# Buffers and loads of the last rows' stacks, places of the bias copies, and low addresses for x's extra stacks, in a linear-attention block with a gated feed-forward part

## The chip, the cores and the metric

One core of one Trainium2 chip. The time is that of the device for one launch, in microseconds (us), lower is better; the number compared is the median over runs of the same kernel. Each engine of the core (PE for matmuls with PEld for its weight loads, DVE, ACT, POOL) works through its own list of instructions in order; SP issues most of the DMA transfers, in order as well.

## What is computed

```python
S, D, F, H = 2048, 576, 4608, 32
xn = layernorm(x)
q, k, v = split(xn @ wqkv)                       # 32 heads of 18
pq, pk = phi(q), phi(k)                          # phi(t) = (t > 0 ? t + 1 : exp(t)) + 1e-6
s = ((pq @ (pk.T @ v)) / (pq @ sum(pk) + 1e-6)) @ wo
g = silu(gelu(xn @ w1 + b1) @ w2 + b2)           # 576 -> 4608 -> 576
out = x + s * g
```

All in float32. The two big products, `xn @ w1` and its result `@ w2`, are nearly all of the work.

## The kernel before

**Numbers.** A product of float32 matrices is made of three matmuls: each operand is split into a high part that the PE takes as it is (`..h`, a cast on ACT) and a low part (`..l`, a subtraction on DVE), and high by high, high by low and low by high are added. On top of that, blocks of 2 by 2 are multiplied with seven products in place of eight, so operands are also sums and differences of blocks. Such sums are computed on POOL and DVE, split, and stored to DRAM for the second half of the rows (`op..` stores, `w..<-op` loads).

**Stages.** From 0 to about 283 us of the profiled execution run the layernorm, the projections and the attention; its result goes to DRAM. The rest is the feed-forward part: 18 *chunks*, two halves of the 2048 rows by nine pieces of F of 512 columns (`half`, `c`). A chunk has 28 *steps* of about 1.6 us of PE work. Steps 0 to 13 are two `Up` (the first product, seven each, into PSUM tiles `a`, `b`, `zy`, `e`). Steps 14 to 27 are the second product: seven products 1, 2, 7, 4, 5, 3, 6 of two steps each (`pm`, L1461), whose results DVE adds to `macc` (the sums of the output, which start from the bias `b2`). Between the two, ACT applies bias and gelu (`g`, L1307), and casts the h operands. For product i and half j of its depth these are tile `(i, j)`. Their buffers are five pairs of tiles, first written in a chunk so: h0 by (1,0) at step 7, h2 by (2,0) at step 9, h4 by (7,0) at step 10, h1 by (1,1) at step 11, h3 by (2,1) at step 12. `mid` is a tile of five blocks for intermediate sums of an `Up` (L1316, L1319, L1322) and of `W1`. `b<-e,mid` (L1325) is the sum that PE's step 12 (`e<-xSH,wb`) waits for, since it takes over the tile of `e`.

**Order.** On DVE, ACT, POOL and PE the program's order is kept. It comes from tables: `add(base + at, f)` puts a call of `f` at step `at` of a chunk. A list by steps decides thus what stands before what on an engine; a call at a negative step is one of the chunk before. SP's order is set by the scheduler. Each of its transfers uses one of eight semaphores in turn, so it starts only after the transfer eight places ahead has landed.

**Last rows.** D = 576 is 4 x 128 + 64. The last 64 rows of x and of the weights are stacked two blocks on top of each other, so that one more matmul closes a product: `xrest` (of x) against `w.rest(i)` (of the weights). The stacks are made from raw rows by class `Rest`: `hi` casts (L333), `lo` subtracts (L337), `sums` forms block sums of the raw rows on DVE (L354 or L356), `store` writes h and l to DRAM (L348), each twice over. There are two groups: the first has 3 blocks (128 x 384), the second, of the sums, 4 (128 x 512). Stacks 0 and 1 of the weights are made in the attention stage (`REST_PLAN`: round and slot of the four calls), the others in chunks 2, 3, 5 and 6 by `Rest2` (`plan_rest2`), which borrows h buffers: h4's high tile for the raw rows, h2 for the first group, h1 for the second. These instructions bear names such as `rs2Falseh1l`: stack 2, not of x, buffer h1, low part. Back from DRAM come x's stacks as `x_extra` (1 MB, four of seven; once for each half) and the weights' as `we` (448 KB for each `Up`, L1083).

**Memory.** Pools open from the low or the high end (`side="right"`) of the on-chip memory. The slot "mid" at a low address holds the attention's `scr` in the first stage, and becomes free when its last round is done with it; then it holds `mid`. `x_extra` and `we` lie on the right side.

**Biases.** `set_bias` copies `b2` on ACT into the four quarters of `macc` (L1279), in chunks 0 and 9.

Of the kernel before, what the change touches and what calls it, by code (L numbers as in the profile page):

```python
# [8 lines left out]
F32 = mybir.dt.float32  # L9
F32R = mybir.dt.float32r  # L10
# [5 lines left out]
P = 128  # L16
# [29 lines left out]
def linear_attention_gated_ffn(ctx, tc, x, wqkv, wo, w1, w1e, b1, w2, b2, out):  # L46
    nc = tc.nc
# [35 lines left out]
    def stage(cols, name):  # L83
        t = stg.tile([P, D], F32, tag="stg", name=name)
        return t[:, :cols]
# [25 lines left out]
    xp = ctx.enter_context(tc.tile_pool(name="xp", bufs=1, reuse_waits="tile"))  # L111
# [6 lines left out]
    scr = xp.tile([P, 2560], F32, tag="mid", name="scr")  # L118
# [7 lines left out]
    we_dram = [dram.tile([P, 4, 7, P], F32, name=f"we_dram{i}") for i in range(NB4)]  # L126
# [19 lines left out]
    class Weight:  # L146
# [8 lines left out]
        def rest(self, n):  # L155
            hs = slice(n * HD, (n + 1) * HD)
            return self.rh[:, hs], self.rl[:, hs]
# [157 lines left out]
    class Rest:  # L315
# [9 lines left out]
        def tiles(self, g):  # L325
            pool, bufs = rest_pool
            t = pool.tile([P, 2, 4 * P], F32R, tag="re", name=f"re{self.i}{self.of_x}{g}", bufs=bufs)
            return t[:, 0], t[:, 1]
# [258 lines left out]
    def add(step, fn, *args):  # L587
        plans.setdefault(step, []).append((fn, args))
# [19 lines left out]
    DV, GP = nc.vector, nc.gpsimd  # L608
# [85 lines left out]
    def plan_pair(p):  # L694
# [103 lines left out]
    rests, rest_pool = {}, (t1, 1)  # L798
    REST_PLAN = {
# [3 lines left out]
    }  # L803

    def load_rows(key):
# [14 lines left out]
    for p in range(1, NPAIR):  # L820
        plan_pair(p)
        base = p * NSP
# [22 lines left out]
    def q_tiles(r):  # L845
        return [r_bufs[(2 * r + s) % 4] for s in range(2)]
# [11 lines left out]
    base = NPAIR * NSP  # L858
# [173 lines left out]
    class W1:  # L1032
# [11 lines left out]
        def T(self, i):  # L1044

            a, b = slice(0, 2), slice(2, 4)
            f0, f1, src = self.f0, self.f1, self.src
            tt = EW1.tensor_tensor
            if i in (5, 6):
                at = (i - 5) * 2 * P  # L1050
                t = mid[:, 4, at : at + 2 * P] if self.n else scr[:, at : at + 2 * P]
                src[i] = t.rearrange("p (k c) -> p k c", k=2)
            if i == 5:
                tt(src[5], f1[:, a], f0[:, a], op=SUB)  # L1054
            elif i == 6:
                tt(src[6], f1[:, b], src[5], op=SUB)
            elif i == 7:
                src[7] = f1[:, a]
                tt(src[7], f1[:, b], f1[:, a], op=SUB)
            else:  # L1060
                src[4] = f0[:, b]
                tt(src[4], f0[:, b], src[6], op=SUB)
# [16 lines left out]

        def load_rest(self):  # L1080
            n = self.n % NP
            self.re = xe.tile([P, 7, P], F32R, tag="we", name=f"we{self.n}", bufs=2)
            nc.sync.dma_start(self.re.bitcast(F32), we_dram[n // 4][:, n % 4])  # L1083

        def rest(self, i):
            return self.re[:, W_REST[i]]

    W1_K = {"a": KM, "b": 2, 4: 2, 5: 2, 6: 2, 7: 2}

# [17 lines left out]
    W_REST = {1: 0, 2: 1, 3: 2, 5: 3, 4: 4, 6: 5, 7: 6}  # L1107
# [9 lines left out]
    w1t, w2_raw0 = {}, []  # L1117
# [5 lines left out]
    for r in range(NPAIR + 2):  # L1123
        base = (NPAIR + r) * NSP
# [3 lines left out]
        if r < NPAIR:  # L1128
            a, b = q_tiles(r)
# [15 lines left out]
        if 1 <= r < NPAIR:  # L1145
            a, b = q_tiles(r)
            at = base + 2 * (r == 2)
# [12 lines left out]
        if 3 <= r <= 7:  # L1160
            n = 2 * r + 3
# [25 lines left out]
        if 1 <= r < NPAIR:  # L1187
            for s in range(2):
                at = Attend(r - 2, s) if r >= 2 else None
# [14 lines left out]
        elif r == NPAIR:  # L1204
            w = w1t[0]
            at = Attend(r - 2, 0)
# [6 lines left out]
            at = Attend(r - 2, 1)  # L1213
# [12 lines left out]
        elif r > NPAIR:  # L1226
            for s in range(2):
                at = Attend(r - 2, s)
# [14 lines left out]

    gp = ctx.enter_context(tc.tile_pool(name="gp", bufs=1, side="right", reuse_waits="tile"))
    xe = ctx.enter_context(tc.tile_pool(name="xe", bufs=1, side="right", reuse_waits="tile"))
    x_extra = xe.tile([P, 4, 4, P], F32R, name="x_extra")

    def load_x_extra(i):
        nc.sync.dma_start(x_extra.bitcast(F32), xe_dram[i][:, :, :4])

    load_x_extra(0)
    for n in range(2):
        w1t[n].load_rest()
    for d, t in kept:
        nc.sync.dma_start(d, t)
    kept = None
    xrest = {k: t[:, at] for k, (t, at, _) in X_OVER.items()}
    xrest |= {k: x_extra[:, :, j] for j, k in enumerate(X_EXTRA)}
# [3 lines left out]
    tails = {}  # L1262
    macc = fl.tile([P, QH, 5, HD], F32, name="macc")
    C11, C12, C21, C22, U1 = range(5)
    mid = xp.tile([P, 5, 512], F32, tag="mid", name="mid")
    m1_sb, u1_sb, u2_sb = (mid[:, i, :] for i in range(3))

    BIAS = (C11, C22)
# [71 lines left out]
    class Rest2(Rest):  # L1340
# [5 lines left out]
            return gp.tile([P, 512], F32R, tag=tag, name=f"rs{self.i}{self.of_x}{tag}", bufs=1)  # L1346

        def tiles(self, g):
            return [self.tile(f"h{2 - g}{v}") for v in "hl"]

    REST_CHUNK = {2: (2, False), 3: (3, False), 5: (1, True), 6: (4, False)}

    def plan_rest2(base, key):
        def load():
            rests[key] = Rest2(*key)

        add(base + 0, load)
        for at, what, *args in (
            (2, "hi", 0), (3, "lo", 0), (3, "sums", DV), (4, "store", 0), (5, "hi", 1), (6, "lo", 1), (7, "store", 1),
        ):  # L1360
            add(base + at, lambda what=what, args=args: getattr(rests[key], what)(*args))

# [175 lines left out]
    def finish_load(t, h, tiles):  # L1538
        b, q = divmod(t - 8, QH)
        cs = slice(h * HD, (h + 1) * HD)  # L1540
        nc.sync.dma_start(tiles[0], c_dram[b, :, q, h])
        nc.sync.dma_start(tiles[1], s_dram[t, :, cs])
        nc.sync.dma_start(tiles[2], x[t * P : (t + 1) * P, cs])

    def finish(t, h, tiles):
        ct, st, xt = tiles
        nc.gpsimd.tensor_tensor(st, ct, st, op=MUL)  # L1547
        nc.gpsimd.tensor_tensor(st, st, xt, op=ADD)
        nc.sync.dma_start(out[t * P : (t + 1) * P, h * HD : (h + 1) * HD], st)
# [60 lines left out]
    NS = 28  # L1610
# [3 lines left out]
    def plan_w1(add, w, base, T, hi, lo):  # L1614
        for table, what in ((T, w.T), (hi, w.hi), (lo, w.lo)):
            for i, at in table.items():
                add(base + at, what, i)
# [3 lines left out]
        hi={"a": 0, 6: 1, 7: 2, 5: 3, "b": 4, 4: 4},  # L1621
        lo={"a": 0, 6: 1, 7: 2, 5: 3, "b": 4, 4: 4},
# [3 lines left out]
        hi={"a": 24, 6: 25, 7: 26, 5: 26, "b": 27, 4: 27},  # L1626
        lo={"a": 24, 6: 25, 7: 26, 5: 26, "b": 27, 4: 27},
# [10 lines left out]
        hi={  # L1638
            (1, 0): 7, (2, 0): 9, (7, 0): 10, (1, 1): 11, (2, 1): 12, (7, 1): 15, (4, 0): 16,
            (4, 1): 17, (5, 1): 18, (5, 0): 19, (6, 0): 20, (3, 0): 21, (3, 1): 22, (6, 1): 23,  # L1640
        },
        lo={
            (1, 0): 9, (2, 0): 10, (7, 0): 11, (1, 1): 12, (2, 1): 13, (7, 1): 15, (4, 0): 16,
            (4, 1): 17, (5, 1): 18, (5, 0): 19, (6, 0): 20, (3, 0): 21, (3, 1): 22, (6, 1): 23,
        },
# [11 lines left out]
    for step in range(n_chunks):  # L1657
        half, c = divmod(step, NC)
        base = step * NS
        plain = step == n_chunks - 1  # L1660
        h = HOps(c)
        if c == 0:
            if half:
                add(base + 5, load_bias, nc.gpsimd)
            for at, m in zip((10, 11, 13, 14) if half else (5, 6, 7, 8), (C11, C21, C22, C12)):
                add(base + at, set_bias, m)
        if half == 0:
            plan_w1(add, w1t[2 * step + 1], base, **P1)
# [7 lines left out]
            if step == 0:  # L1676
                for i, at in W2_SUMS_FIRST.items():
                    add(at, w2t[0].load, i)
        if half == 0 and c in REST_CHUNK:
            plan_rest2(base, REST_CHUNK[c])  # L1680
        if half == 0 and c < NC - 1:
            add(base + 0, make, W1, w1t, 2 * step + 2)
            add(base + 4, make, W1, w1t, 2 * step + 3)
# [56 lines left out]
        if half == 1 and 1 <= c <= 8:  # L1740
            for k in range(2):
                tiles = {}
                def load(k=k, t=7 + c, tiles=tiles):
                    tiles[0] = finish_tiles(k)
                    finish_load(t, k, tiles[0])
                add(base, load)
                add(base + 4, lambda k=k, t=7 + c, tiles=tiles: finish(t, k, tiles[0]))
# [12 lines left out]
        for j in range(CF // 2):  # L1760
            n = 2 * step + j
# [55 lines left out]
```

## Time and profile before

| what | value |
|---|---|
| median of 3 runs | 1130.23 us (1130.0 to 1131.81) |
| profiled execution, its time / its span | 1133.79 us / 1132.1 us |
| granted PE clock, mean | 0.99 |
| PE busy | 1101.4 us, 97% |
| PEld, DVE, ACT, POOL busy | 90%, 73%, 46%, 40% |
| DMA | 295.02 MB, mean 261 GB/s |
| chain that ended last | PE 82%, DMA 6%, DVE 5%, ACT 4% |

How to read it. A busy time counts an engine's own instructions. The chain is the row of work that set the end, followed back from the last instruction. In an answer by time a row gives start and length in us, the engine, the line, output and inputs, and in brackets how long the engine had been idle and what released it. "DMA x<-y" as a releaser is a transfer that had to land. The granted clock is the share of full speed that the chip let PE have; PE's busy time contains what a lower clock adds.

### The profile page before, as it was taken

What the parts mean: (1) busy time and instruction counts of PE and PEld (TensorE: products, weight loads), DVE (VectorE), ACT (ScalarE), POOL (GpSimd) and SP (SyncE); (2) the same over time, 40 slices, a digit from 0 to 9 for tenths busy, and PEclk for the clock granted to TensorE, in tenths of its full rate; (3) what the DMA queues carried; (4) which work ended last, traced back from release to release, by engine and by line L of the source; (5) the groups of instructions that cost most, each with busy time, mean ns of one, the idle gap of its engine ahead of it and who ended that gap; (6) DMA issues with size and microseconds to landing.
All of it is one profiled execution on the core that took longest, in us unless ns stands there. A gap on an engine that the chain in (4) does not pass through costs nothing.

```text
span 1132.1 us, 18955 instructions
## 1 busy us (share of the span) xinstructions
PE 1101.4 (97%) x6888; PEld 1014.0 (90%) x6888; DVE 822.8 (73%) x1284; ACT 516.7 (46%) x945; POOL 454.3 (40%) x423
## 2 busy tenths in 40 slices
PE   8999999999899989999898999999999999999998
PEld 8999999999698877989788898898998988989988
DVE  6777477996687868788888888675574664755776
ACT  7776455554635434444444435443243242332342
POOL 6854524555345333452524444234132342341310
PEclk9999999999999989999999999999999999999999
DMA  5989838888978969697887969997767667767343
GB/s 203 322 285 335 279 89 282 288 324 288 375 251 295 321 206 348 229 355 230 295 308 240 354 170 360 388 346 251 267 213 234 217 221 225 220 219 223 101 152 115
DMA packets 115867, 295.02 MB, mean 261 GB/s; under 512 B 12221, under 2 KB 31421, under 8 KB 113727
## 3 DMA queue, kind: packets, MB, share of 16 engines
q1 hardware_dynamic: 110207, 282.32, 70.5%
q0 software_dynamic: 4992, 10.32, 5.3%
q8 instruction: 54, 0.88, 0.3%
q10 hardware_dynamic: 576, 1.18, 0.3%
q14 instruction: 38, 0.31, 0.1%
HBM read 180.39 MB, written 108.66 MB: 255 GB/s over the span
## 4 chain that ended last, share of the span: by engine, by line
PE 82%; DMA 6%; DVE 5%; ACT 4%; issue 2%; POOL 0%; SPq 0%; DVEq 0%; ACTq 0%; POOLq 0%
PE pm L1461 34%; PE e L1299 8%; PE zy L1299 8%; PE a L1299 8%; PE pl L477 5%; PE b L1299 4%; PE ps_s L997 4%; PE e L421 2%; PE a L421 2%; PE z L421 2%; PE pd L1576 2%; PE ps_kva L530 1%; DMA we_dram<-rs2Falseh1l 1%; PE b L421 1%; DMA w__8337<-op 1%
## 5 line engine op out<-in xcount | busy, mean ns | idle before, releaser
L1027 ACT CAST h_h<-g 128x512 fp32r<-128x512 f32 x204 | 120.5, 621 | 158.2 <-PE pm L1461 138.9
L1030 DVE TENSOR_TENSOR h_l<-g,h_h 128x512 fp32r<-128x512 f32 x204 | 160.2, 785 | 10.3 <-ACT g L1307 7.4
L1469 DVE TENSOR_TENSOR macc<-macc,pm 128x576 f32<-128x576 f32 x136 | 102.2, 751 | 39.7 <-PE pm L1461 39.6
L1299 PE MATMUL a<-xH,wa 128*128 128x512 f32 x288 | 102.0, 395 | 0.0
L1471 DVE TENSOR_TENSOR macc<-pm,macc 128x576 f32<-128x576 f32 x98 | 74.1, 757 | 25.7 <-PE pm L1461 24.1
L1429 POOL TENSOR_TENSOR mid<-g 128x512 f32<-128x512 f32 x34 | 44.5, 1308 | 105.7 <-ACT g L1307 105.6
L1307 ACT ACTIVATE g<-b,b1c 128x512 f32<-128x512 f32 x36 | 24.8, 689 | 126.0 <-DVE b L1325 125.9
L1299 PE MATMUL e<-xSH,wb 128*128 128x512 f32 x144 | 53.7, 414 | 14.7 <-DVE b L1325 14.6
L1316 ACT COPY mid<-a 128x512 f32<-128x512 f32 x36 | 21.2, 589 | 97.7 <-PE a L1299 97.7
L1299 PEld LDWEIGHTS a<-xH,wa 128*128 128x128 f32 x288 | 54.0, 187 | 12.1 <-ACT mid L1316 0.8
L1423 POOL TENSOR_TENSOR g<-g 128x512 f32<-128x512 f32 x34 | 49.6, 1460 | 32.3 <-DVE h_l L1030 30.9
L1319 DVE TENSOR_TENSOR mid<-b,mid 128x512 f32<-128x512 f32 x36 | 24.7, 685 | 46.1 <-ACT h_h L1027 20.7
L1426 POOL TENSOR_TENSOR g<-g 128x512 f32<-128x512 f32 x34 | 51.7, 1519 | 12.5 <-DVE h_l L1030 11.1
L1299 PE MATMUL a<-xL,wa 128*128 128x512 f32 x144 | 56.2, 390 | 0.0
L1547 POOL TENSOR_TENSOR fin1l<-fin1h,fin1l 128x288 f32<-128x288 f32 x8 | 6.5, 808 | 118.6 <-DMA fin1l<-s_dram 61.8
L1299 PE MATMUL zy<-xH,w 128*128 128x512 f32 x144 | 51.8, 401 | 0.0
L1299 PE MATMUL b<-xSH,w 128*128 128x512 f32 x144 | 50.4, 390 | 0.0
L1299 PE MATMUL zy<-xSH,w 128*128 128x512 f32 x144 | 50.3, 390 | 0.0
L1299 PE MATMUL e<-xSH,w 128*128 128x512 f32 x144 | 50.3, 390 | 0.0
L1299 PEld LDWEIGHTS e<-xSH,wb 128*128 128x128 f32 x144 | 28.3, 196 | 23.8 <-DVE b L1325 17.5
L1420 POOL TENSOR_TENSOR g<-g 128x512 f32<-128x512 f32 x34 | 47.5, 1398 | 2.7
L1054 POOL TENSOR_TENSOR mid<-w1raw 128x256 f32<-128x256 f32 x17 | 13.9, 820 | 85.5 <-DMA w1raw<-w 52.1
(974 smaller groups left out, 3694.1 us busy)
## 6 DMA issues: line engine op xcount, KB each, us to landing
op<-w SPq DMA_DIRECT2D x72, 256.0 KB
w<-op SPq DMA_DIRECT2D x72, 256.0 KB
we<-we_dram SPq DMA_DIRECT2D x36, 448.0 KB
w2raw<-w SPq DMA_DIRECT2D x10, 1152.0 KB
op<-w2o SPq DMA_DIRECT2D x19, 576.0 KB
w1raw<-w SPq DMA_DIRECT2D x18, 512.0 KB
op_a<-wa SPq DMA_DIRECT2D x18, 512.0 KB
wa<-op_a SPq DMA_DIRECT2D x18, 512.0 KB
```

Of the source, the lines that this page charges most:

```text
L421: nc.tensor.matmul(ps, st, mv, start=first and n == 0, stop=n == len(seq) - 1, skip_group_check=True,)
L477: nc.tensor.matmul(self.ps[n], st, self.wk(hl, k, n), start=(i == 0), stop=(i == n_all - 1))
L997: nc.tensor.matmul(self.ps[h], st[:, k, :], w[:, k, h * HD : (h + 1) * HD], start=(i == 0), stop=(i == len(self.seq) - 1),)
L1027: nc.scalar.copy(pair[0], src)
L1030: eng.tensor_tensor(pair[1], src, pair[0].bitcast(F32), op=SUB)
L1299: nc.tensor.matmul(ps.rearrange("p (c j) -> p c j", c=4), st, mv, start=first and n == 0, stop=n == len(seq) - 1, skip_group_check=True,)
L1420: tt(src[5, pr], A(1, 1), A(1, 0), op=SUB)
L1423: tt(src[6, pr], src[5, pr], A(0, 0), op=ADD)
L1426: tt(src[3, pr], src[6, pr], A(0, 1), op=SUB)
L1461: nc.tensor.matmul(ps[:, q, :HD], hs[p][st][:, cs], m[:, p, :], start=(n == 0 and i not in CHAIN), stop=(n == len(seq) - 1), skip_group_ch ...
L1469: nc.vector.tensor_tensor(dst, dst, src, op=SUB)
L1471: nc.vector.tensor_tensor(dst, src, dst, op=ADD)
```

## The change

Four parts, as the diff has them.

1. `Rest2` takes h1 for the first group and h3 for the second (before: h2 and h1). Its raw rows are asked for four steps before the chunk (before: at step 0), its first store comes at step 3, ahead of the sums (before: 4), the second at step 6 (before: 7). `store`, `hi`, `lo`, `sums` themselves stay.
2. The four bias copies of chunk 0 go from steps 5, 6, 7, 8 to 10, 11, 13, 14, where chunk 9 has its own.
3. A tile `low` of 20 blocks of 128 takes the low slot. Its first 16 blocks are `x_extra`; the last four hold, two for each of two `Up` in turn, two of the seven blocks of `we` (those of products 1 and 2). The other five stay on the right side. So a `load_rest` is two transfers, 128x256 and 128x640, in place of one of 128x896; there are 36 of these loads. `mid` moves to the right side, and the first W1's sums go to a staging tile, since `scr` was their place.
4. `REST_PLAN` starts the stacks 0 and 1 of the weights about a round earlier in the attention stage.

```diff
@@ the attention stage
-        (0, False): ((10, 12), (11, 6), (12, 6), (13, 6)),
-        (1, False): ((12, 12), (13, 6), (14, 6), (15, 6)),
+        (0, False): ((9, 12), (10, 11), (11, 6), (12, 6)),
+        (1, False): ((11, 12), (12, 11), (13, 6), (14, 6)),
@@ W1.T
             if i in (5, 6):
+                if i == 5:
+                    self.tmp = mid[:, 4] if self.n else stage(4 * P, "w1t0")
                 at = (i - 5) * 2 * P
-                t = mid[:, 4, at : at + 2 * P] if self.n else scr[:, at : at + 2 * P]
+                t = self.tmp[:, at : at + 2 * P]
@@ W1.load_rest, W1.rest
-            self.re = xe.tile([P, 7, P], F32R, tag="we", name=f"we{self.n}", bufs=2)
-            nc.sync.dma_start(self.re.bitcast(F32), we_dram[n // 4][:, n % 4])
+            a = xe.tile([P, 5, P], F32R, tag="we", name=f"we{self.n}", bufs=2)
+            b = low[:, 16 + 2 * (n % 2) :][:, :2]
+            nc.sync.dma_start(b.bitcast(F32), we_dram[n // 4][:, n % 4, :2])
+            nc.sync.dma_start(a.bitcast(F32), we_dram[n // 4][:, n % 4, 2:])
+            self.re = a, b
...
-            return self.re[:, W_REST[i]]
+            at = W_REST[i]
+            return self.re[1][:, at] if at < 2 else self.re[0][:, at - 2]
@@ after the attention
-    x_extra = xe.tile([P, 4, 4, P], F32R, name="x_extra")
+    low = xp.tile([P, 20, P], F32R, tag="mid", name="low")
+    x_extra = low[:, :16].rearrange("p (c k) j -> p c k j", k=4)
...
     load_x_extra(0)
-    for n in range(2):
-        w1t[n].load_rest()
+    mid = xe.tile([P, 5, 512], F32, name="mid")
+    w1t[0].load_rest()
     for d, t in kept:
         nc.sync.dma_start(d, t)
+    w1t[1].load_rest()
...
-    mid = xp.tile([P, 5, 512], F32, tag="mid", name="mid")
@@ Rest2.tiles
-            return [self.tile(f"h{2 - g}{v}") for v in "hl"]
+            return [self.tile(f"h{1 + 2 * g}{v}") for v in "hl"]
@@ plan_rest2
-        add(base + 0, load)
+        add(base - 4, load)
-            (2, "hi", 0), (3, "lo", 0), (3, "sums", DV), (4, "store", 0), (5, "hi", 1), (6, "lo", 1), (7, "store", 1),
+            (2, "hi", 0), (3, "lo", 0), (3, "store", 0), (3, "sums", DV), (5, "hi", 1), (6, "lo", 1), (6, "store", 1),
@@ the chunks
-            for at, m in zip((10, 11, 13, 14) if half else (5, 6, 7, 8), (C11, C21, C22, C12)):
+            for at, m in zip((10, 11, 13, 14), (C11, C21, C22, C12)):
...
-        if half == 0 and c in REST_CHUNK:
-            plan_rest2(base, REST_CHUNK[c])
+        if half == 0 and c + 1 in REST_CHUNK:
+            plan_rest2(base + NS, REST_CHUNK[c + 1])
```

What stands in a row on an engine. DVE in chunk 2, around the two low parts of stack 2 (`rs2False..`), before; `w_..` are low parts of weights, L1325, L1332 and L1336 the sums of an `Up`:

```order
L1325 TENSOR_TENSOR b4_4701<-e4_4703,mid_3677 128x512
L1030 TENSOR_TENSOR w5_5_4766<-mid_3677,w5_5_4766 128x256
L1030 TENSOR_TENSOR w2_2__4771<-w2raw2_4351,w2_2__4771 128x576
L337 TENSOR_TENSOR rs2Falseh2l_4754<-rs2Falseh4h_4719,rs2Falseh2h_4753 128x384
L356 TENSOR_TENSOR rs2Falseh4h_4719<-rs2Falseh4h_4719 128x128 x4
L1030 TENSOR_TENSOR wb_5_4790<-w1raw5_4293,wb_5_4790 128x256
L1030 TENSOR_TENSOR w4_5_4792<-w1raw5_4293,w4_5_4792 128x256
L1030 TENSOR_TENSOR w2_2__4800<-w2s7_2_4305,w2_2__4800 128x576
L1332 TENSOR_TENSOR e4_4703<-e4_4703,mid_3677 128x512
L1336 TENSOR_TENSOR zy4_4702<-zy4_4702,mid_3677 128x512
L1030 TENSOR_TENSOR w2_2__4836<-w2raw2_4351,w2_2__4836 128x576
L337 TENSOR_TENSOR rs2Falseh1l_4820<-rs2Falseh4h_4719,rs2Falseh1h_4819 128x512
```

and now (the kernel's later lines have moved down by seven):

```order
L1332 TENSOR_TENSOR b4_4710<-e4_4712,mid_3661 128x512
L337 TENSOR_TENSOR rs2Falseh1l_4755<-rs2Falseh4h_4628,rs2Falseh1h_4754 128x384
L356 TENSOR_TENSOR rs2Falseh4h_4628<-rs2Falseh4h_4628 128x128 x4
L1030 TENSOR_TENSOR w5_5_4780<-mid_3661,w5_5_4780 128x256
L1030 TENSOR_TENSOR w2_2__4785<-w2raw2_4357,w2_2__4785 128x576
L1030 TENSOR_TENSOR wb_5_4799<-w1raw5_4298,wb_5_4799 128x256
L1030 TENSOR_TENSOR w4_5_4801<-w1raw5_4298,w4_5_4801 128x256
L1030 TENSOR_TENSOR w2_2__4809<-w2s7_2_4310,w2_2__4809 128x576
L1339 TENSOR_TENSOR e4_4712<-e4_4712,mid_3661 128x512
L1343 TENSOR_TENSOR zy4_4711<-zy4_4711,mid_3661 128x512
L337 TENSOR_TENSOR rs2Falseh3l_4827<-rs2Falseh4h_4628,rs2Falseh3h_4826 128x512
L1030 TENSOR_TENSOR w2_2__4846<-w2raw2_4357,w2_2__4846 128x576
```

The first low part and the four sums have moved up in front of two weight subtractions, to stand right behind `b<-e,mid`; the second low part has changed places with one weight subtraction.

SP in chunk 3, among the stores of the weights: `op..` are stores of split weight operands, `w1raw` and `w2s` loads of raw weights and raw sums for later chunks. Before:

```order
L1024 DMA op_5_5289<-w_7_5286 128x512
L1024 DMA op_1_5294<-w_3__5291 128x1152
L1024 DMA op_b<-wb_5310 128x512
L1024 DMA op_4_5318<-w_7_5312 128x512
L1024 DMA op_7_5323<-w_3__5320 128x1152
L348 DMA we_dram_109<-rs3Falseh2h 128x2x384
L348 DMA we_dram_109<-rs3Falseh2l 128x2x384
L1038 DMA w1raw_5327<-w 128x1024
L1377 DMA w2s_4_5342<-w 128x576
L1024 DMA op_3_5359<-w_3__5356 128x1152
L348 DMA we_dram_109<-rs3Falseh1h 128x2x512
L348 DMA we_dram_109<-rs3Falseh1l 128x2x512
```

and now:

```order
L348 DMA we_dram_109<-rs3Falseh1h 128x2x384
L348 DMA we_dram_109<-rs3Falseh1l 128x2x384
L1024 DMA op_5_5305<-w_7_5302 128x512
L1024 DMA op_1_5310<-w_3__5307 128x1152
L1024 DMA op_b<-wb_5321 128x512
L1024 DMA op_4_5329<-w_7_5323 128x512
L1024 DMA op_7_5334<-w_3__5331 128x1152
L1038 DMA w1raw_5336<-w 128x1024
L1384 DMA w2s_4_5351<-w 128x576
L348 DMA we_dram_109<-rs3Falseh3h 128x2x512
L348 DMA we_dram_109<-rs3Falseh3l 128x2x512
L1024 DMA op_3_5371<-w_3__5368 128x1152
```

The first two stores of the stack (128x2x384) stand in front of five `op` stores that they stood behind; the second two (128x2x512) have passed one `op` store, and still stand behind `w1raw` and `w2s`.

ACT in chunk 0, around the four copies into `macc` (`e`, `zy`, `a`, `b` are PSUM tiles of the two `Up`, `h_h` the high parts of h), before:

```order
L1307 ACTIVATE g<-e_3683,b1c 128x512
L1279 COPY macc<-macc 128x3x288
L1307 ACTIVATE g<-zy_3682,b1c 128x512
L1279 COPY macc<-macc 128x4x288
L1316 COPY mid<-a_3809 128x512
L1279 COPY macc<-macc 128x3x288
L1027 CAST h_h<-g 128x512
L1279 COPY macc<-macc 128x4x288
L1027 CAST w_0__3837<-w2raw_3434 128x576
L1027 CAST w_0__3851<-w2raw_3434 128x576
L1027 CAST h_h<-g 128x512
L1307 ACTIVATE g<-b_3810,b1c 128x512
```

and now:

```order
L1027 CAST w_0__3837<-w2raw_3434 128x576
L1027 CAST w_0__3851<-w2raw_3434 128x576
L1027 CAST h_h<-g 128x512
L1314 ACTIVATE g<-b_3811,b1c 128x512
L1286 COPY macc<-macc 128x3x288
L1027 CAST h_h<-mid 128x512
L1314 ACTIVATE g<-a_3810,b1c 128x512
L1286 COPY macc<-macc 128x4x288
L1027 CAST h_h<-g 128x512
L1314 ACTIVATE g<-e_3813,b1c 128x512
L1027 CAST h_h<-g 128x512
L1314 ACTIVATE g<-zy_3812,b1c 128x512
```

The four copies stand no more between `zy` of the first `Up` and the cast of the weights, but after the gelu of `b` of the second `Up`, two of them ahead of the cast of (1,1).

## Prediction

> **What bounds the kernel now.** I read the page first: the span, and the row of the granted clock in 40 slices of 28.3 us.
>
> ```profile
> span 1132.1 us, 18955 instructions
> PEclk9999999999999989999999999999999999999999
> ```
>
> PE is the bound nearly everywhere, so only places where PE stands still or runs slowly can be gained. The 8 near 400 us says that the clock fell there. Next I cut the span at the starts of the feed-forward chunks, read from the chain (each run of `pm` products ends where the next chunk starts). The rows are chunks 0, 2, 3, 4, 5, 6 and 9; columns: stretch, length, busy time of PE, PEld, DVE, ACT, POOL, granted clock, DMA share, GB/s.
>
> ```profile
> 282.87:333.25 50.38, 46.66 (x266) 41.51 (x265) 36.05 (x54) 27.92 (x50) 18.94 (x18) 0.97 0.89 316
> 378.18:431.75 53.57, 48.42 (x268) 43.36 (x267) 39.94 (x62) 22.41 (x43) 19.63 (x19) 0.94 0.79 272
> 431.75:481.89 50.14, 47.17 (x268) 41.90 (x267) 40.26 (x62) 22.32 (x43) 20.63 (x19) 0.97 0.81 285
> 481.89:526.83 44.94, 44.94 (x267) 40.79 (x267) 37.63 (x56) 21.32 (x41) 20.43 (x19) 1.00 0.82 283
> 526.83:577.21 50.38, 47.03 (x267) 41.75 (x267) 41.67 (x62) 22.41 (x43) 20.81 (x19) 0.97 0.84 288
> 577.21:627.65 50.44, 47.06 (x267) 41.80 (x267) 41.60 (x62) 22.41 (x43) 20.34 (x19) 0.97 0.84 285
> 717.53:763.88 46.35, 45.24 (x267) 40.80 (x267) 31.52 (x41) 22.46 (x32) 16.24 (x12) 1.00 0.98 367
> ```
>
> Chunk 4 is a full one, 44.94 us with PE never idle. Over it the others have 5.44 (chunk 0), 8.63, 5.20, 5.44, 5.50 (chunks 2, 3, 5, 6) and 1.41 (chunk 9). Each excess has two parts: PE idle (chunk 2: 53.57 - 48.42 = 5.15) and PE busy longer at a fallen clock (48.42 - 44.94 = 3.48). So every stall of some us is paid again: 1.7 us in chunk 0, 2.2 in 3, 2.1 in 5 and 6. Chunks 2, 3, 5 and 6 are those with the last rows' stacks: 24.77 us in all. Their waits, on ACT (chunk 2 twice, 3 twice, 5, 6):
>
> ```profile
> 398.99 0.62 ACT L1027 CAST h_h<-g 128x512 fp32r<-128x512 f32 x1 [4.14 <-DMA we_dram<-rs2Falseh2h]
> 405.32 0.62 ACT L1027 CAST h_h<-g 128x512 fp32r<-128x512 f32 x1 [3.91 <-DMA we_dram<-rs2Falseh1h]
> 451.60 0.62 ACT L1027 CAST h_h<-g 128x512 fp32r<-128x512 f32 x1 [3.18 <-DMA we_dram<-rs3Falseh2h]
> 457.85 0.62 ACT L1027 CAST h_h<-g 128x512 fp32r<-128x512 f32 x1 [2.88 <-DMA we_dram<-rs3Falseh1h]
> 552.59 0.62 ACT L1027 CAST h_h<-g 128x512 fp32r<-128x512 f32 x1 [1.18 <-DMA xe_dram<-rs1Trueh1h]
> 603.33 0.62 ACT L1027 CAST h_h<-g 128x512 fp32r<-128x512 f32 x1 [1.37 <-DMA we_dram<-rs4Falseh1h]
> ```
>
> A stored stack still occupies the buffer in which the next h is wanted. The low part of the second stack lands later yet, as the chain shows for chunks 2 and 3 (start, us): at 406.53 and 459.05.
>
> ```profile
> 397.01 9.52 DMA we_dram<-rs2Falseh1l
> 450.85 8.20 DMA we_dram<-rs3Falseh1l
> ```
>
> **The stacks, chunk 2.** Two stalls. The first, at step 12, is DVE's. These rows are DVE's of chunk 2, then the one of chunk 4 that answers to 398.89:
>
> ```profile
> 386.41 0.42 DVE L1030 TENSOR_TENSOR w<-mid,w 128x256 fp32r<-128x256 f32 x1 [1.05 <-ACT w L1027]
> 387.66 0.55 DVE L337 TENSOR_TENSOR rs2Falseh2l<-rs2Falseh4h,rs2Falseh2h 128x384 fp32r<-128x384 f32 x1
> 388.24 1.27 DVE L356 TENSOR_TENSOR rs2Falseh4h<-rs2Falseh4h 128x128 f32<-128x128 f32 x4
> 393.88 1.40 DVE L1030 TENSOR_TENSOR w__4836<-w2raw,w__4836 128x576 fp32r<-128x576 f32 x1 [1.81 <-ACT w__4836 L1027]
> 395.21 1.77 DVE L337 TENSOR_TENSOR rs2Falseh1l<-rs2Falseh4h,rs2Falseh1h 128x512 fp32r<-128x512 f32 x1
> 398.89 0.69 DVE L1325 TENSOR_TENSOR b<-e,mid 128x512 f32<-128x512 f32 x1
> 499.64 0.70 DVE L1325 TENSOR_TENSOR b<-e,mid 128x512 f32<-128x512 f32 x1 [0.31 <-PE e L1299]
> ```
>
> `b<-e` runs 17.75 us after the start in chunk 4 and 20.71 after it in chunk 2: 2.96 late. The order puts the first low part and the sums (0.55 + 1.27) into the 1.05 us wait, and the second low part (1.77) into the 1.81 us wait. Added 3.59, filled 2.86: about 0.7 us late, of which `e<-xSH,wb` on PE bears some 0.5 (2.96 late made a stall of about 2.4). I take 0.3 for chunks 2 and 3. In 5 and 6 DVE has 1.7 us more to do (41.67 against 39.94): between 0.3 and 1.9, and 0.6 taken, since DVE waits elsewhere too.
>
> The first store goes to buffers wanted at step 11 and passes five transfers in the queue; that wait ends. The second is closer. Its buffer moves from step 11 to step 12, so from product 1 to product 2, two of 28 steps or 3.2 us later. But it goes on the way hardly sooner: the queue still puts it behind the raw weights and `w2s`, each transfer waits until the eighth before it has landed, and only one store of 0.6 MB is no longer ahead of it. In this stretch the transfers run without a gap (first the queue's row of that store, then 384 to 388 us):
>
> ```profile
> 395.72 0.45 SPq L1024 DMA_DIRECT2D op<-w__4836  x1
> 384.00:388.00 4.00, 4.00 (x19) 3.27 (x18) 2.22 (x5) 2.61 (x6) 0.00 (x0) 1.00 1.03 406
> ```
>
> 0.6 MB at 406 GB/s is 1.5 us, so I let both halves land 1.5 us sooner: chunk 2 at 403.8 and 405.0. When does PE want them? Chunk 9 shows it: there PE stopped five matmuls into product 1 (163 of 168 come after), which begins half a chunk, 22.5 us, after 717.53, at 740.0, and wanted the low part some 0.65 us later.
>
> ```profile
> 738.52 1.15 ACT L1279 COPY macc<-macc 128x1152 f32<-128x1152 f32 x1
> 740.22 1.61 DVE L1030 TENSOR_TENSOR h_l<-g,h_h 128x512 fp32r<-128x512 f32 x1 [0.85 <-ACT h_h L1027]
> 741.88 22.00 PE pm L1461 x163
> ```
>
> So product 2's low part is wanted at 22.5 + 3.2 + 0.65 = 26.35 after the start, plus the 0.3 of step 12: 404.8 in chunk 2. The buffer is free at 405.0 and the subtraction takes 0.7: 0.9 late. In chunk 3: landed at 459.05 - 431.75 = 27.3, less 1.5, plus 0.7, is 26.5 against 26.65: 0.1 taken, for scatter. Chunk 6 I put at 0.2, chunk 5 at 0. Ends: nothing; or no sooner landing at all (rival 1). ACT casts that h some 3 us before PE wants it and stands still for that long at most; behind it lie `g<-zy` and the h of product 7, wanted 3.2 us later still.
>
> No stall left is near those that made the clock fall. After the change: 1.2, 0.4, 0.6 and 0.8 us of 24.77; gain 21.8. The number of loads, casts, sums and stores stays.
>
> **Bias copies of chunk 0.** First and last of four on ACT, then DVE:
>
> ```profile
> 295.41 0.91 ACT L1279 COPY macc<-macc 128x864 f32<-128x864 f32 x1
> 299.64 1.17 ACT L1279 COPY macc<-macc 128x1152 f32<-128x1152 f32 x1
> 298.46 0.69 DVE L1319 TENSOR_TENSOR mid<-b,mid 128x512 f32<-128x512 f32 x1 [3.07 <-ACT mid L1316]
> 301.42 1.38 DVE L1030 TENSOR_TENSOR w__3837<-w2raw,w__3837 128x576 fp32r<-128x576 f32 x1 [2.27 <-ACT w__3837 L1027]
> 305.06 0.69 DVE L1325 TENSOR_TENSOR b<-e,mid 128x512 f32<-128x512 f32 x1
> ```
>
> `b<-e` comes 22.2 us after 282.87, 4.4 later than in chunk 4, and the four copies are about 4.2 of ACT's time ahead of it. Moved, they leave one extra weight subtraction (about 1.2, against chunk 4) there: 0.6 at step 12. At steps 10 to 14 two copies lie ahead of an h of product 1, as in chunk 9, whose rows stand above and whose excess is 1.41, 1.2 of it this stop. So 5.44 becomes 1.9: 3.5 gained (ends: nothing left, 5.4; as long a stop as before, 0). Chunk 9 has its copies there already and keeps its 1.41.
>
> **The passage to the feed-forward part.** The queue, the chain, ACT, PE's first use:
>
> ```profile
> 261.27 0.52 SPq L1249 DMA_DIRECT2D x_extra<-xe_dram  x1
> 263.91 7.71 DMA op<-w2o
> 271.68 4.17 DMA w1raw<-w
> 275.93 0.62 ACT L1027 CAST wa<-w1raw 128x512 fp32r<-128x512 f32 x1 [4.30 <-DMA w1raw<-w]
> 278.31 0.54 PE L997 MATMUL ps_s<-kw_h,th 128*128 128x288 f32 x2 [1.18 <-ACT th L971]
> L1299 PEld LDWEIGHTS a<-x_extra,we x1: 186/186/186, 284.0 to 284.0; 128*128 128x128 f32 x1
> ```
>
> `x_extra` (1 MB, 2.6 us at 400 GB/s) leaves its place ahead of the `op` stores and a `we` part of 0.33 MB takes it: 1.8 us sooner for what follows, so ACT's 4.30 shrinks and PE's 1.18 goes: 1.2 gained. `x_extra` now starts after the raw weights; two `w1raw` of 0.5 MB, `w2raw` of 1.2 and `x_extra`, 3.2 MB from about 271 on, are 8 us, landing at about 280 against 282.8 wanted. If the margin of 2.8 is wrong by as much again, some 3 us are lost. The `re1False` stores that leave the last round cost or give nothing: ahead of that gap PE waits for nothing there.
>
> **36 more DMAs** (each `we` in two). SP's issue takes 0.3 to 0.5 us each (261.27: 0.52), at most 18 us of queue time over 18 chunks, a us in each; PE never waits for `we` in chunk 4, so I take 0, with ends of 0 and the 2 us of rival 2. The Trainium skill ("SBUF — State Buffer", The DMA setup-cost knee) fits a transfer as about 2 us plus its bytes at 436 GB/s and so advises the largest single transfers. By that the split would add 2 us to each, 4 in a chunk. The trace disagrees for a full queue: transfers of 0.25 to 0.6 MB went through at 406 GB/s together, where the fit gives a lone one of 0.26 MB about 100.
>
> **The sum.** 1.2 + 3.5 + 21.8 = 26.5. The profiled execution took 1133.79 us (span 1132.1), 3.56 over the median of 1130.23; the gain should carry over, so 1103.7, stated as 1104 (span about 1105.6).
>
> **Rivals.** 1. The second stacks land no sooner, since the queue is bound by bytes. Late by my rule: 2.4 in chunk 2, 1.4 in 3, and, with the low part landing 1.2 after the high one as in 2 and 3 and DVE's 0.6, 0.7 in 5 and 1.1 in 6; in all 5.6 against 1.2 taken, so 1108; with the clock falling behind each for 1.7, 1115. For it: the gapless 1.03 share. Against: the store no longer ahead. The Trainium skill ("TensorE: Matmul & The Clock Gate", Part 1) says that the rate halves after at least one idle window of about 3.4 us; by that such stalls never bring the clock down and 1108 would be the end of it. The trace disagrees: chunk 3 stood still 2.97 us in all and still lost 2.2 more.
>
> 2. DMA becomes the bound. Chunk 2's DMA share is 0.79 x 53.57 = 42.3 us of work, chunks 5 and 6 the same; in 45.6 us that is 0.93. If the extra DMAs cost their 2 us of all engines, 4 a chunk, the four here overflow by 0.7 each and chunk 9 (45.4 of work) by 3: about 6 lost, 1110. Against: chunk 9 ran at 0.98 with 367 GB/s.
>
> 3. Slower: each transfer waits for the eighth before it, and the small `we` parts now take two more of those places in a chunk, so fewer bytes are on the way and weights arrive late in all chunks. Place: PE's first step of each Up. To eat up 26.5 it must cost 1.6 us in each of 17 chunks; at 2 us, 1138. Against: chunk 4 has 18% of its transfer time free, and the second half asks for `we` long ahead.
>
> 4. Everything clears: 31.4 gained with the passage, 1099.
>
> **How the numbers follow.** Forecast 0.57, rival 1 0.17, rival 2 0.08, rival 3 0.06, rival 4 0.10, and 0.02 for some part undone by an unseen wait. A measurement here tells 0.2% (2.3 us) from no change. Faster: the first three and the fourth rival, 0.91; within 0.2%: 0.03, that 0.02 and a tail of rival 2; slower 0.06. The range runs from rival 4 less a us, 1098, to the dear end of rival 1 and 2 us more, 1117; the forecast alone would be 1100 to 1108.
>
> **What would show it.** Right: no ACT wait on an `rs` transfer at a product 1 buffer; chunks 3 to 6 at 45.3 to 45.8 us, chunk 2 near 46, chunk 0 near 46.8; the clock at 1.00 from 300 to 660 us. Wrong: a wait of PE on the h of product 2 over 1 us, PE waiting for `x_extra` at the first Up, chunks of the second half over 44.94, or a new clock drop in chunk 0.

## The result, and the profile after

The changed kernel took 1116.18 us (median of 4 runs, 1114.53 to 1118.75) against 1130.38 (4 runs): 0.9874 of the time before, 95% interval 0.9853 to 0.9895. On a second chip (e9) it was 1117.18 against 1133.65, 0.9849 (0.9826 to 0.9873). So the direction was right, the range of 1098 to 1117 just held the time, and of the 26.5 us forecast some 14 came. The profiled execution is the fastest of its four, 1114.53 us; that of before had been slower than its median. The two spans therefore differ by more, 19.3 us, and what follows counts in spans.

The page after, span and granted clock; no slice shows an 8 any more:

```profile
span 1112.8 us, 19015 instructions
PEclk9999999999999999999999999999999999999999
```

The stretches of chunks 0, 2, 3, 4, 5, 6 and 9, in the columns used before:

```profile
281.38:328.74 47.36, 45.63 (x268) 40.78 (x267) 36.63 (x54) 27.55 (x50) 20.04 (x17) 1.00 0.96 334
373.60:421.10 47.50, 45.50 (x267) 40.88 (x267) 40.39 (x62) 22.15 (x43) 21.88 (x19) 1.00 0.89 307
421.10:468.46 47.36, 45.29 (x267) 40.74 (x267) 40.31 (x62) 22.15 (x43) 21.40 (x19) 1.00 0.87 302
468.46:513.30 44.84, 44.84 (x268) 40.80 (x267) 37.64 (x56) 21.33 (x41) 20.19 (x19) 1.00 0.83 284
513.30:560.35 47.05, 45.23 (x268) 40.86 (x267) 39.30 (x62) 22.14 (x43) 21.07 (x19) 1.00 0.89 309
560.35:609.27 48.92, 46.60 (x267) 42.32 (x267) 40.13 (x62) 22.12 (x43) 20.74 (x19) 0.97 0.84 293
698.97:745.02 46.05, 45.39 (x267) 40.79 (x267) 33.63 (x41) 22.65 (x32) 16.51 (x12) 1.00 1.00 377
```

Chunks 2, 3, 5 and 6 still have 2.2 to 4.1 us over a full one. They gave 6.07, 2.78, 3.33 and 1.52 (the lengths before less these), in all 13.7 of the 21.8 forecast. PE's first product of the first Up begins at 281.22 in place of 282.34, so the passage gave 1.1 and chunk 0, counted from there, 3.4: as forecast, 1.2 and 3.5. A full chunk is now 44.84 in place of 44.94, which nobody had forecast.

What is left in chunk 2, row by row on ACT, DVE (three rows) and PE:

```profile
398.97 0.62 ACT L1027 CAST h_h<-g 128x512 fp32r<-128x512 f32 x1 [2.39 <-DMA we_dram<-rs2Falseh3h]
396.88 0.69 DVE L1343 TENSOR_TENSOR zy<-zy,mid 128x512 f32<-128x512 f32 x1
400.09 0.69 DVE L1030 TENSOR_TENSOR h_l<-g,h_h 128x512 fp32r<-128x512 f32 x1 [2.53 <-DMA we_dram<-rs2Falseh3l]
400.70 1.41 DVE L1478 TENSOR_TENSOR macc<-pm,macc 128x576 f32<-128x576 f32 x2
401.51 0.53 PE L1468 MATMUL pm<-w__4567,h_h 128*128 128x288 f32 x2 [1.71 <-DVE macc L1478]
```

By its row PE does not wait for the h of product 2 here (e2 tests this). It waits for DVE's `macc<-pm`, the eviction of product 1 (L1478), and that stands on DVE behind the subtraction that waits for the store. Product 2 goes on adding in the PSUM bank that product 1 left (`CHAIN = {2: 1, ...}`, matmuls without a fresh start), so it may begin only when product 1 has been read out of it. The same releaser stands at the other three stops:

```profile
448.89 0.53 PE L1468 MATMUL pm<-w__5089,h_h 128*128 128x288 f32 x2 [2.07 <-DVE macc L1478]
540.77 0.40 PE L1468 MATMUL pm<-w__6115,h_h 128*128 128x288 f32 x1 [1.82 <-DVE macc L1478]
588.30 0.85 PE L1468 MATMUL pm<-w__6637,h_h 128*128 128x288 f32 x2 [2.32 <-DVE macc L1478]
```

And the chain has the stores of these stops (start, length):

```profile
391.85 8.15 DMA we_dram<-rs2Falseh3l
439.75 7.63 DMA we_dram<-rs3Falseh3l
530.97 8.29 DMA xe_dram<-rs1Trueh3l
577.67 8.26 DMA we_dram<-rs4Falseh3l
```

They land 26.4, 26.3, 26.0 and 25.6 us after their chunk's start: the 1.9 and 1.0 us sooner that the two chunks whose rows were shown gained are about the 1.5 forecast. So the landing was forecast well, and the time at which it is wanted was not.

**Theory A**: the stack's store holds DVE, behind it the eviction, behind that PE. **B**: PE waits for the operand itself. **C**: these chunks are slow by DVE's extra work or by full transfers, whatever the buffers.

### The profile page after: what moved, and what is told of

It reads as the page before. It is cut to its first block, busy times and chain, and to the rows that moved or that the text cites. A ratio compares the mean times of both kernels' runs of the same rounds, so it can differ in the third digit from the quotient of the medians.

```text
span 1112.8 us, 19015 instructions
## 1 busy us (share of the span) xinstructions
PE 1091.2 (98%) x6888; PEld 1008.3 (91%) x6888; DVE 822.9 (74%) x1284; ACT 515.6 (46%) x945; POOL 459.6 (41%) x423
## 3 DMA queue, kind: packets, MB, share of 16 engines
q10 hardware_dynamic: 576, 1.18, 0.3%
## 4 chain that ended last, share of the span: by engine, by line
PE 85%; DMA 5%; DVE 5%; ACT 3%; issue 2%; POOL 1%; SPq 0%; DVEq 0%; POOLq 0%; ACTq 0%
PE pm L1468 33%; PE a L1306 8%; PE zy L1306 8%; PE e L1306 8%; PE ps_s L997 5%; PE b L1306 5%; PE pl L477 5%; PE e L421 3%; PE a L421 2%; PE z L421 2%; PE pd L1583 2%; PE ps_kva L530 1%; DMA c_dram<-macc 1%; DVE h_l L1030 1%; PE b L421 1%
## 5 line engine op out<-in xcount | busy, mean ns | idle before, releaser
L1030 DVE TENSOR_TENSOR h_l<-g,h_h 128x512 fp32r<-128x512 f32 x204 | 168.9, 828 | 13.3 <-ACT g L1314 3.1
L1478 DVE TENSOR_TENSOR macc<-pm,macc 128x576 f32<-128x576 f32 x98 | 73.7, 756 | 20.4 <-PE pm L1468 19.2
L1436 POOL TENSOR_TENSOR mid<-g 128x512 f32<-128x512 f32 x34 | 46.8, 1375 | 92.1 <-ACT g L1314 92.1
L1306 PE MATMUL e<-xSH,wb 128*128 128x512 f32 x144 | 50.6, 392 | 0.5 <-DVE b L1332 0.5
L1427 POOL TENSOR_TENSOR g<-g 128x512 f32<-128x512 f32 x34 | 47.4, 1393 | 2.7
L1314 ACT ACTIVATE g<-e,b1c 128x512 f32<-128x512 f32 x36 | 24.8, 689 | 40.5 <-DVE e L1339 40.4
```

The source lines that it names most:

```text
L1030: eng.tensor_tensor(pair[1], src, pair[0].bitcast(F32), op=SUB)
L1306: nc.tensor.matmul(ps.rearrange("p (c j) -> p c j", c=4), st, mv, start=first and n == 0, stop=n == len(seq) - 1, skip_group_check=True,)
L1314: nc.scalar.activation(g, ps, AF.Gelu_apprx_tanh, bias=b1c[:, f : f + 1])
L1478: nc.vector.tensor_tensor(dst, src, dst, op=ADD)
```

## Experiments on the stop at product 2

**e1: the buffer is free at once.** The second store takes its bytes from a tile of x that is only read in that half, so the stacks stored are wrong.

```diff
+        def store(self, g):
+            if g:
+                self.t[g] = [x_tiles[0][:, 0, :4]] * 2
+            super().store(g)
```

> Second store of the stacks takes as many bytes from a tile of x that nothing writes then, so h3 is free at once; the stacks stored are wrong, the work and the bytes are the same. Theory A (h of (2,1) waits for the store's landing on DVE, and the eviction of product 1, on whose PSUM bank product 2 adds up, stands behind it on DVE): the four stops at product 2 of 2.0, 2.4, 2.1 and 2.6 us go, and the 1.4 of lowered clock in chunk 6: 1106 to 1109. Theory B (PE waits for the operand h itself, no matter for the eviction): the same here. Theory C (the chunks with stacks are slow by DVE's extra work or by full transfers, not by the buffer): stays within 2 us of 1116.

Measured: 1104.87 us (1103.99 to 1107.14), ratio 0.9744 (0.9719 to 0.9768), a little under the expected range. Chunks 2 and 3:

```profile
373.33:418.49 45.16, 45.15 (x268) 40.74 (x267) 40.06 (x62) 22.24 (x43) 20.89 (x19) 1.00 0.87 300
418.49:463.33 44.84, 44.84 (x267) 40.80 (x267) 38.96 (x62) 22.24 (x43) 20.88 (x19) 1.00 0.87 296
```

PE is busy all through, with the same bytes moved. C falls: the four stops were the buffer's, worth about 11 us between the medians (1116.18 and 1104.87, on two chips).

**e2: the eviction ahead of the wait.**

```diff
+                    if what == "lo" and (i, pr) == (2, 1) and half == 0 and c in REST_CHUNK:
+                        at = 14
```

> In the four chunks with stacks, the subtraction for (2,1) stands behind the first eviction of product 1 on DVE in place of before it; the store lands as before. Theory A: PE starts product 2 on time and stops only where it wants the low part of (2,1) and the second eviction: stops of about 2.0 become 1.0 to 1.2 each, 1111 to 1113. Theory B: PE waits for the same landing, nothing gained: 1115 to 1117.

Measured: 1110.55 us (1110.25 to 1111.77), 0.9794 (0.977 to 0.9818). DVE and PE in chunk 2:

```profile
398.54 0.76 DVE L1478 TENSOR_TENSOR macc<-pm,macc 128x576 f32<-128x576 f32 x1 [0.68 <-PE pm L1468]
400.89 0.69 DVE L1030 TENSOR_TENSOR h_l<-g,h_h 128x512 fp32r<-128x512 f32 x1 [1.59 <-ACT g L1314]
401.63 0.40 PE L1468 MATMUL pm<-w__4567,h_l 128*128 128x288 f32 x1 [0.77 <-DVE h_l L1030]
```

With the store landing no sooner, two instructions changed about save 6 us. PE now starts product 2 at once and stops inside it, for the low part: in the four chunks 0.77, 0.81, 1.06 and 0.40 in place of 1.71, 2.07, 1.82 and 2.32. So it was the order on DVE's queue that held the start of product 2, and B, which had nothing gained, falls; what is left of the stop is a wait for the operand. Another stop comes up later in chunks 2 and 3, at product 4 (408.87, 1.24 us by PE's row; its cause was not followed): the gain is not the whole one.

**e3: the store sooner.**

```diff
-(5, "hi", 1), (6, "lo", 1), (6, "store", 1),
+(4, "hi", 1), (4, "lo", 1), (4, "store", 1),
```

> Cast, subtraction and store of the second group at step 4 in place of 5 and 6: the store passes five transfers (1.9 MB, some 4.7 us at 400 GB/s) and lands near 21.7 us after the chunk's start in place of 26. Theories A and B: no stop at product 2, 1106 to 1109; where DVE is now late at step 12, up to 0.5 us for each of four chunks more. Theory C: 1116.

Measured: 1106.5 us (1105.36 to 1108.42), 0.9754 (0.973 to 0.9779), as A and B expect. The stores of the second group leave at 385 in place of 391 us (the queue's rows), and no wait of PE, DVE, ACT or POOL on them is left in the four chunks. Chunk 2:

```profile
385.10 0.37 SPq L348 DMA_DIRECT2D we_dram<-rs2Falseh3h  x1
385.83 0.84 SPq L348 DMA_DIRECT2D we_dram<-rs2Falseh3l  x1
```

This kernel leaves nothing out and is about 10 us faster than the change.

## Experiments on the parts

**e4: the stacks as before, the rest of the change kept** (the four hunks on `Rest2` and `plan_rest2` undone).

> Buffers and steps of the stacks as in the kernel before, the other three parts kept. By the two profiles the stacks carry 13.7 of the 19.3 us between the spans, so the other parts are worth 5 to 6: 1124 to 1126. If the parts lean on each other (the low tiles' transfers make the stores land sooner or later), it lies outside 1122 to 1128.

Measured: 1129.09 us (1124.92 to 1132.93) against 1133.25: 0.9951 (0.9934 to 0.9969). The other three parts together bring 4 us, less than the 5 to 6 expected; the stacks are most of the change. The time lies outside 1122 to 1128, but the kernel before was slower on this chip too, 1133.25 in place of 1130.38. Counted as a gain, 4.2 is inside what those bounds meant (2.4 to 8.4), so it does not show that the parts lean on each other.

**e10: the stacks alone, on the kernel before.**

> The kernel before with the stacks' part of the change alone. If the parts add up: before less 4.2 (e4) is the others, so this one is some 4 us above the changed kernel, 1118 to 1122. The stop of 1.2 us ahead of the feed-forward part, which was gone with either the low tile (e7) or the earlier stacks (e5), should be there again, and chunk 0's stop at step 12 with a fallen clock too.

Measured: 1119.62 us (1117.71 to 1123.57) against 1133.65: 0.9876 (0.9855 to 0.9897); the changed kernel beside it (e9) 1117.18. So on top of the stacks the other parts bring some 2.4, with intervals that overlap. The stop ahead of the feed-forward part is there again, smaller (0.46 against 1.18 before, though nothing of the edit lies ahead of it), and chunk 0 is long again, with a stop of 3.72 us at step 12:

```profile
277.58 0.54 PE L997 MATMUL ps_s<-kw_h,th 128*128 128x288 f32 x2 [0.46 <-ACT th L971]
282.40:332.32 49.92, 46.20 (x265) 41.28 (x264) 36.10 (x54) 27.64 (x49) 18.71 (x18) 0.97 0.88 315
```

**e9: the change again**, for the comparison above.

> The changed kernel once more, beside the kernel before and the two that follow on one chip: 1114 to 1119, 0.985 to 0.989 of before. Its four stops of 2.0 to 2.6 us at product 2 lie at the edge of what brings the clock down, so its times should scatter more than those of the kernels without them (1103.6 to 1105 in e8).

Measured: 1113.70 to 1120.11 us, mean granted clocks from 0.998 (the fastest) to 0.993 and 0.995 (the two slowest); e3's runs stay within 1105.36 to 1108.42. As expected.

The next five start from e3, where little is left that scatters.

**e5: the low tile undone** (part 3; x's extra stacks and whole `we` tiles on the right side, `mid` in the low slot).

> The kernel of e3 (1106.5) with the low tile undone: x's extra stacks and whole we tiles on the right side, mid in the low slot, 36 transfers fewer. Theory: the passage gets its stop of 1.2 us back (raw weights behind x_extra), and the 0.10 us that every undisturbed chunk lost with the change (44.94 to 44.84) comes back, 1.7 over 18: 1109 to 1110. Rival (the chunks became shorter for another reason, run or chip): 1107 to 1108. Rival (36 transfers cost time): under 1106.

Measured: 1105.39 us (1104.79 to 1107.14), 0.976 (0.9739 to 0.9781): no 3 us were lost, so in the sum the theory is wrong. By its number the rival on the 36 transfers (under 1106) would hold, but e7, on the same chip and with these transfers, took 1104.69, so no cost of theirs is shown. The two halves of the theory can be read in the trace one by one. The shorter chunk is the low tile's: chunk 10, e3 first, e5 second:

```profile
736.23:781.06 44.83, 44.83 (x267) 40.79 (x267) 28.04 (x38) 14.47 (x24) 15.01 (x13) 1.00 0.79 267
735.46:780.40 44.94, 44.94 (x268) 40.79 (x267) 28.06 (x38) 14.48 (x24) 15.03 (x13) 1.00 0.78 268
```

But the passage keeps its gain without the low tile, so that was not the move of `x_extra` alone (e7 shows it with the low tile and without the earlier stacks). And e5 lacks two stops of e3's profile: 0.38 us at step 12 of chunk 5, which e6, e7, e8 and e11 have as well, and 0.67 in chunk 7, which none of these has, so that this one is not the low tile's. Chunk 5 of e3 is 45.49, that of e5 44.94:

```profile
508.03:553.52 45.49, 45.11 (x268) 40.72 (x267) 40.01 (x62) 22.34 (x43) 21.03 (x19) 1.00 0.92 314
509.21:554.15 44.94, 44.94 (x267) 40.79 (x267) 38.66 (x62) 22.25 (x43) 20.73 (x19) 1.00 0.92 320
```

In chunk 5 of e3, POOL's sums of `W1` start at 518.74, 10.7 us after the chunk's start and between DVE's subtractions; in e5 at 520.58, 11.4 after it, when the last of these has begun. The same DVE subtraction and the POOL sum beside it, e3 and e5:

```profile
519.66 0.81 POOL L1058 TENSOR_TENSOR mid<-w1raw,mid 128x256 f32<-128x256 f32 x1
519.78 1.30 DVE L1030 TENSOR_TENSOR w__6363<-w2s,w__6363 128x576 fp32r<-128x576 f32 x1
520.38 0.75 DVE L1030 TENSOR_TENSOR w__6350<-w2s,w__6350 128x576 fp32r<-128x576 f32 x1
520.58 1.15 POOL L1054 TENSOR_TENSOR mid<-w1raw 128x256 f32<-128x256 f32 x1 [6.82 <-DVE w L1030]
```

So the low tile gives 0.1 in each chunk, 1.7 in all, and the medians do not show it. Part is given back in chunk 5. In some executions more goes where the rows of x change over to the second half: there PE waits for `x_extra` in `low`, 0.24, 0.26 and 0.79 us in the profiles of e6, e7 and e11, and 1.36 in that of e9. PE's own row names a load of weights; its weight load, at the same time, names the transfer of `x_extra`:

```profile
702.11 0.19 PEld L1306 LDWEIGHTS a<-low 128*128 128x128 f32 x1 [1.79 <-DMA low<-xe_dram]
702.11 0.50 PE L1306 MATMUL a<-low 128*128 128x512 f32 x1 [1.36 <-DMA w<-op]
```

**e6: the bias copies of chunk 0 at steps 5 to 8 again.**

> The kernel of e3 with chunk 0's bias copies at steps 5 to 8 again. Chunk 0 went from 5.44 to about 2.5 us over a full chunk with the change: back to 5.4, 1109 to 1110. Rival (chunk 0 gained from the earlier raw weights, not from the copies): 1106 to 1107.

Measured: 1109.46 us (1107.46 to 1111.1), 0.9792 (0.9768 to 0.9816); 4 to 5 us over e5 and e7 on the same chip, 3 over e3. In the profile chunk 0 is 3.0 us longer than in e3 (50.47 against 47.45 from its first product). The copies are what made chunk 0 long, by PE's stop at step 12:

```profile
304.53 0.80 PE L1306 MATMUL e<-xSH,wb 128*128 128x512 f32 x1 [3.76 <-DVE b L1332]
```

**e7: the attention stage's stacks at their rounds of before.**

> The kernel of e3 with the attention stage's two stacks at their rounds of before. Theory: nothing, 1106 to 1107. Rival (part of the shorter passage is theirs, as 1 MB of stores leaves the last round): 1107.5 to 1108.

Measured: 1104.69 us (1104.17 to 1106.39), 0.9754 (0.9732 to 0.9775): nothing lost, as the theory has it, or a little won; no stop ahead of the feed-forward part. In the profiles either of the two parts alone was enough to end that stop. How much that is worth is open: e9, with both parts, and e10, with neither, begin the first product at 281.58 and 281.61.

**e8: the bias copies late, at 14, 17, 15, 19.** One of them now reads a quarter of `macc` that an eviction has changed, so these sums are not the reference's; the work is the same.

> The kernel of e3 with the bias copies of chunks 0 and 9 at steps 14, 15, 17, 19, behind ACT's casts of (1,1) and (2,1) and ahead of the evictions that need them. Theory: the stop of 1.4 us at product 1 of chunk 0 and of 1.2 in chunk 9 go: 1103.5 to 1104.5. Rival (chunk 9 stops for its full transfers, chunk 0 for its second weight subtraction): 1105.5 to 1106.5.

Measured: 1104.62 us (1103.59 to 1105.01), 0.9749 (0.9728 to 0.977). In the profile chunk 0 is 0.7 shorter than in e3; chunk 9 is 0.6 shorter and still stops, with no copy ahead of it on ACT. PE's stop, ACT's wait before it, POOL's rows before that, and the same POOL sum in chunk 10:

```profile
712.75 0.41 PE L1468 MATMUL pm<-w__8255,h_l 128*128 128x288 f32 x1 [1.16 <-DVE h_l L1030]
709.13 0.62 ACT L1027 CAST h_h<-mid 128x512 fp32r<-128x512 f32 x1 [1.52 <-POOL mid L1436]
707.21 0.57 POOL L1280 DMA_DIRECT2D macc<-b  x1 [8.27 <-DMA c_dram<-macc]
707.80 1.30 POOL L1436 TENSOR_TENSOR mid<-g 128x512 f32<-128x512 f32 x1
747.59 1.30 POOL L1436 TENSOR_TENSOR mid<-g 128x512 f32<-128x512 f32 x1 [3.33 <-ACT g L1314]
```

So in this kernel the stop in chunk 9 comes from POOL's sum, which starts 19.3 us after the chunk's start, against 12.8 in chunk 10. It stands on POOL behind the reload of `b2` into `macc` for the second half (L1280), which waited for a store of `macc` to land: again a store that holds an in-order engine, and what stands behind it. No run without that reload tests it. The prediction had read the stop as the copies' price; in the kernel before, ACT had no wait on POOL at this place, so there the copies may have been it.

**e11: the copies at 14 and 15, all ahead of the first eviction that changes what they read, and e7's rounds.**

```diff
-zip((10, 11, 13, 14), (C11, C21, C22, C12))
+zip((14, 14, 15, 15), (C11, C21, C22, C12))
```

> The kernel of e3 with the bias copies of chunks 0 and 9 at steps 14 and 15 (all four ahead of the first eviction that changes what they read) and the attention stage's stacks at their rounds of before. Theory: chunk 0 some 0.5 and chunk 9 some 0.6 us shorter than in e3, the last nothing: 1104 to 1105.5.

Measured: 1106.31 us (1105.12 to 1106.93), 0.9754 (0.9736 to 0.9773): no better than e3. The four copies hold ACT in one piece, and chunk 0 stops later, for an h (chunk 9 too, 0.80 us at 724.42):

```profile
306.45 3.83 ACT L1286 COPY macc<-macc 128x864 f32<-128x864 f32 x4
315.57 0.50 PE L1468 MATMUL pm<-w__3779,h_h 128*128 128x288 f32 x2 [0.87 <-ACT h_h L1027]
```

The best versions that leave nothing out are e3, e5, e7 and e11, which the intervals do not tell apart: 0.975 to 0.976 of before.

## Why the prediction was right and wrong

- **Its own signs.** Of those for right, two came: no ACT wait on an `rs` transfer at a product 1 buffer, and chunk 0 at 47.4 near its 46.8. The other sizes failed: 47.36, 47.05 and 48.92 us in chunks 3, 5 and 6 against 45.3 to 45.8, 47.50 in chunk 2 against 46, and a granted clock of 0.97 in chunk 6. Of those for wrong one came, a wait of PE over 1 us at product 2, but not on its h.
- **Where the time sits** (the four chunks with stacks, chunk 0, the passage): right. **First stalls, at step 12**: right, none of the four is left in the changed kernel, the 0.3 to 0.6 allowed for them did not come.
- **Second stalls: the step that failed.** "So product 2's low part is wanted at 26.35 after the start" took PE's operand as what is wanted. Wanted first is the eviction of product 1, before product 2 starts at 25.7 (22.5 + 3.2). It stands behind the waiting subtraction on DVE, which takes 0.7, and takes 0.7 itself: the buffer had to be free by about 24.3, and came free at 25.6 to 26.4. I followed what stood behind the wait on ACT and left out DVE. Forecast 1.2 us for the stops at product 2 and the clock behind them; the rows show 1.71, 2.07, 1.82 and 2.32 of wait, 7.9 in all, and one fall of the clock. e2 shows that the order on DVE held the start, e1 and e3 that the buffer did it.
- **"No stall left is near those that made the clock fall"**: wrong with it. In chunk 6 the clock fell for 3.41 us as PE took up again (PE's share of the window is the second column):

```profile
585.90:588.30 2.40, 0.09 (x1) 0.00 (x0) 2.28 (x3) 1.14 (x2) 2.32 (x2) 1.00 1.07 413
588.30:591.71 3.41, 3.41 (x14) 3.41 (x15) 2.43 (x3) 0.00 (x0) 3.25 (x4) 0.50 1.02 317
```

- The Trainium skill ("TensorE: Matmul & The Clock Gate", Part 1) asks for at least one idle window of about 3.4 us before the rate halves. The trace disagrees again: PE's wait was 2.32 us. The 3.41 us for which the lower rate lasted agree with the page's window. The waits of 1.7 to 2.1 in chunks 2, 3 and 5 went without a fall. The length of the wait alone does not decide: in e9 waits of 2.08 and 2.01 us (chunks 5 and 6) were followed by a fall and one of 2.25 (chunk 2) was not, nor were two of 2.56 and 2.55 in e10. That agrees with windows that run on by themselves, as the page says, but no run here shows where they begin.
- **Rival 1** gave 1108 to 1115 and so the nearest time, but by a mechanism that did not happen: the stores did land sooner. The upper end of the range came from it, so that the range held the time is luck.
- **Chunk 0**: right in size, and e6 shows the copies as the cause. **Chunk 9 as the price of the new places**: right in number (1.41 forecast, 1.21 over a full chunk seen). The cause is not settled: with the copies moved away (e8) the stop stays, behind POOL's reload of `b2`.
- **The passage**: 1.2 forecast, about 1.1 seen in one pair of profiles and 0.03 between e9 and e10; and either part 3 or part 4 ends the stop (e5, e7), where the prediction had put part 4 at nothing and all on `x_extra`.
- **`x_extra` late at the first Up**: it was not. Late it came, in some executions, at the change of halves, which I had not looked at. **36 more DMAs**: no cost of their own was seen, e5 without them is within 1.1 us of e3.
- **"The gain should carry over" from the profile to the median**: wrong by 5 us: the spans differ by 19.3, the medians by 14.2. The profiled execution of before lay 3.6 above its median, that of after 1.65 below. In the changed kernel the time of an execution goes with its mean granted clock (e9); for the kernel before, its runs do not show it on every chip.

## What to carry to other kernels

A wait moved to a later instruction is paid by whatever stands behind that instruction on the same in-order engine: list the queue of every engine that will stand still, DVE's evictions above all, and ask for each entry when PE wants it. Where a product adds on in the PSUM bank of the one before, the deadline is the eviction's, ahead of the operand's. And when a transfer is late by 1 to 2 us, ask for it sooner first: here that (e3, up to two steps) ended the stops that another buffer had left, and brought 10 us.

## What the runs showed of the hardware

Full chunks took 44.84 us in every kernel with x's extra stacks and part of the weights' extra rows at low addresses, and 44.94 in those without (before, e5, e10), with the same matmuls. In chunk 10 of e3 and e5 the difference lies ahead of the second product: from the chunk's first matmul to its first `pm` it is 22.44 against 22.54 us, and from there to the next chunk's first matmul 22.39 against 22.40. Which of the tiles does it was not separated (`mid` changed its place as well), and why is open.

A DVE subtraction of two operands on chip took 0.75 us where it started ahead of POOL's sum, which then took 1.15, and 1.30 where POOL's sum had started 0.12 us before it (e5 and e3, above). This agrees with the Trainium skill ("SBUF — State Buffer", SBUF: two separate sides): such an instruction and a POOL instruction that reads the same memory do not run at once, the second waits.
